# One program order for all engines, idle products in round 0, and a longer reach for the weights, in a linear-attention and MLP kernel

## The chip, the cores and the metric

The kernel runs on one core of a Trainium2 chip. The metric is the device time of one execution in microseconds; lower is better. Each kernel was run several times beside the kernel before on the same chip.

## The reference, cut to what matters

```python
# r, k, v, w: (4 batches, 8 heads, 768 steps, 48); u: (8, 48)
for t in range(S):
    cur = einsum('bhd,bhe->bhde', u[None] * kt, vt)
    y[:, :, t] = einsum('bhd,bhde->bhe', rt, state + cur)
    state = wt[:, :, :, None] * state + einsum('bhd,bhe->bhde', kt, vt)
x = y.transpose(0, 2, 1, 3).reshape(B, S, 384)
xn = (x - mean) / sqrt(var + 1e-06) * g_ln
out = x + maximum(xn @ w_ch1, 0.0) @ w_ch2      # 384 x 1536 and 1536 x 384, handed over as float64
```

## The kernel before

The work is cut into eight rounds of 384 steps, each of two units of four heads. The recurrence of a round is done in six levels. At each level TensorE multiplies r by k (`a_ps`), then VectorE scales r and k by products of w ("scalings", `grow` in the changed kernel) and keeps a part of `a_ps` by a predicated copy. After the levels come the states (`kv`, `s`), the outputs `y`, a normalization, and the MLP of the round: twelve steps for the first matrix (`h_ps`) and twelve for the second (`o_ps`). The MLP of a round runs on TensorE in the gaps of the next round's levels. A stretch of the loop with one level and its share of MLP steps is called a slot.

The weights come as 64-bit floats in 24 parts of 384 columns, and the kernel makes 32-bit floats of their bits. That is a *conversion*: ScalarE makes two halves, VectorE joins them with three operations, and a last integer add finishes the part.

```python
def weights():                                   # a generator; convert(n) takes n steps of it
    for i, (dst, _) in enumerate(parts):
        fetch(i + 2)                             # DMA of the raw part, three buffers
        ...
        ACT.activation(out=e, in_=hi, func=AF.Abs, scale=2.0**-16)
        ACT.activation(out=low, in_=lo, func=AF.Copy, scale=2.0**-29)
        DVE.tensor_scalar(...)                   # clamp
        DVE.tensor_scalar(...)                   # shift, and
        DVE.scalar_tensor_tensor(...)            # sign
        POOL.tensor_tensor(out=dst.bitcast(I32), in0=e, in1=low, op=ALU.add)
        yield
# ... round 0:
for lev in range(NLEV):
    level(now, lev)
    ...
    convert(2)                                   # 12 of the 24 parts, before the first MLP
# ... later rounds, after each slot:
    convert(3)
```

Only TensorE's instructions are held in program order. The scheduler of the framework places those of the other engines.

## Time and profile before

| stage | length, us | from the trace |
|---|---|---|
| round 0, to the first h_ps | 85.4 | TensorE's clock 0.67 |
| first MLP, to the first h_ps of the second | 96.5 | TensorE busy 88.3 |
| the rest | 446.2 | TensorE full |

The median was 631.82 us, and the profiled span 628.1. The page's first part gives busy time, share of the span and number of instructions of each engine. The view of ScalarE's waits in the second stage has what was waited for, the total in us, how often, and the longest wait:

```profile
PE 573.4 (91%) x8456; PEld 387.2 (62%) x8456; DVE 303.2 (48%) x683; ACT 185.2 (29%) x402; POOL 152.4 (24%) x205
```

```profile
ACT h L475 <- PE h_ps L56: 13.7, 6, 6.3
...
ACT wl L212 <- POOL w_sb L225: 5.5, 1, 5.5
```

ScalarE mostly waits for TensorE's products, which here is no loss. Its half conversion (`wl`) waited for a buffer once.

### The profile page before, as it was taken

Reading aid. Unit: us, or ns where it says so; the run is one execution under the profiler, and the core shown is the slowest. Engines: PE = TensorE matmul, PEld = TensorE weight load, DVE = VectorE, ACT = ScalarE, POOL = GpSimd, SP = SyncE. Lnnn points to the kernel's source line nnn. Section 1 sums busy time; section 2 is a strip of 40 time slices with the busy share of each in tenths; the row PEclk is TensorE's granted clock in tenths of the full one; section 3 lists DMA queues with packets and bytes.
Section 4 is the critical chain, followed back from the end, with each engine's and each line's share of the span. In section 5 each row is a group of like instructions: output and inputs, shape, how many; then the busy total and the mean of one; then the engine's idle time right before and its main releaser. Section 6 shows DMA issues by size and latency. Waiting matters only on the chain.

```text
span 628.1 us, 19238 instructions
## 1 busy us (share of the span) xinstructions
PE 573.4 (91%) x8456; PEld 387.2 (62%) x8456; DVE 303.2 (48%) x683; ACT 185.2 (29%) x402; POOL 152.4 (24%) x205
## 2 busy tenths in 40 slices
PE   5366597989999999999999999999999999999997
PEld 4255465656656766667667666676666666566554
DVE  1598959867563544452646356355226361231000
ACT  4108426352143311531243213331142004301200
POOL 7666737670160013300330005101030000000000
PEclk9556769889999989999999999998999999999999
DMA  7656766803410342013400341002000000000000
GB/s 134 144 105 190 182 124 175 183 14 77 91 48 1 59 94 47 15 39 74 88 15 12 68 99 38 1 16 46 26 15 3 15 15 14 1 15 25 1 13 25
DMA packets 123251, 36.83 MB, mean 59 GB/s; under 512 B 116896, under 2 KB 120096, under 8 KB 123168
## 3 DMA queue, kind: packets, MB, share of 16 engines
q1 hardware_dynamic: 121568, 35.32, 25.4%
q8 instruction: 66, 1.08, 0.7%
q10 hardware_dynamic: 1600, 0.30, 0.3%
q14 instruction: 17, 0.14, 0.1%
HBM read 30.87 MB, written 4.72 MB: 57 GB/s over the span
## 4 chain that ended last, share of the span: by engine, by line
PE 82%; DVE 8%; issue 3%; DMA 2%; POOL 2%; SPq 2%; ACT 1%; POOLq 0%; DVEq 0%; ACTq 0%
PE h_ps L56 30%; PE o_ps L56 29%; PE a_ps L56 10%; PE y L56 4%; PE kv L56 2%; PE r_ps L59 2%; PE kn_ps L59 2%; SPq L112 2%; DVE we L221 1%; PE w_ps L59 1%; PE xT_ps L59 1%; DMA nat_r<-in_r_dram 1%; DVE kT L309 1%; PE k_ps L59 1%; DVE rT L309 1%
## 5 line engine op out<-in xcount | busy, mean ns | idle before, releaser
L56 PE MATMUL h_ps<-xT,w_sb 128*128 128x384 f32 x576 | 202.1, 499 | 2.2 <-ACT h L475 2.2
L56 PE MATMUL o_ps<-w_sb,h 128*128 128x384 f32 x576 | 201.2, 495 | 0.0
L56 PEld LDWEIGHTS h_ps<-xT,w_sb 128*128 128x128 f32 x576 | 107.3, 194 | 66.5 <-issue 4.2
L56 PEld LDWEIGHTS o_ps<-w_sb,h 128*128 128x128 f32 x576 | 106.4, 194 | 61.3 <-issue 3.0
L56 PE MATMUL a_ps<-rT,kT 48*64 48x32 f32 x4608 | 86.8, 229 | 25.8 <-DVE kT L309 20.2
L56 PEld LDWEIGHTS a_ps<-rT,kT 48*64 48x64 f32 x4608 | 81.2, 146 | 37.4 <-issue 19.7
L475 ACT ACTIVATE h<-h_ps 128x384 f32<-128x384 f32 x96 | 47.0, 489 | 114.6 <-PE h_ps L56 111.7
L487 DVE TENSOR_TENSOR o<-o_ps,x 128x384 f32<-128x384 f32 x24 | 13.3, 556 | 118.3 <-PE o_ps L56 118.3
L280 POOL TENSOR_TENSOR vo<-v,own 128x576 f32<-128x576 f32 x16 | 19.5, 1221 | 196.1 <-DMA v<-in_v_dram 123.9
L309 DVE TENSOR_TENSOR kT<-kT,tot 128x384 f32<-128x384 f32 x80 | 60.2, 752 | 0.0
L323 DVE COPY_PREDICATED A<-mask,a_ps 128x384 f32<-128x384 int8 x80 | 54.6, 751 | 0.0
L309 DVE TENSOR_TENSOR rT<-rT,tot 128x384 f32<-128x384 f32 x80 | 49.9, 623 | 4.3 <-PE a_ps L56 2.1
L374 DVE SCALAR_TENSOR_TENSOR s<-s,decay,kv 128x48 f32<-128x48 f32 x160 | 30.4, 258 | 43.7 <-PE kv L56 43.7
L421 DVE TENSOR_TENSOR x<-y,vo 128x576 f32<-128x576 f32 x16 | 12.1, 757 | 61.6 <-PE y L56 61.6
L225 POOL TENSOR_TENSOR w_sb<-we,wl 128x384 int32<-128x384 int32 x24 | 33.7, 1416 | 25.6 <-DVE we L221 22.5
L264 POOL TENSOR_TENSOR rk<-nat_k,nat_r 128x576 f32<-128x576 f32 x16 | 27.1, 1691 | 36.1 <-DMA nat_r<-in_r_dram 17.3
L275 DVE TENSOR_REDUCE own<-rk 128x12 f32<-128x576 f32 x16 | 12.0, 749 | 46.5 <-POOL rk L269 46.5
L460 ACT ACTIVATE xT<-xT_ps,g_sb 128x384 f32<-128x384 f32 x24 | 13.9, 580 | 58.5 <-PE xT_ps L59 58.5
L241 ACT COPY rT<-r_ps 128x384 f32<-128x384 f32 x32 | 14.6, 477 | 50.7 <-PE r_ps L59 50.7
L241 ACT COPY kT<-k_ps 128x384 f32<-128x384 f32 x32 | 14.8, 478 | 43.9 <-PE k_ps L59 43.8
L56 PEld LDWEIGHTS y<-v,A 64*64 64x64 f32 x384 | 21.8, 138 | 8.1 <-issue 7.1
L255 POOL TENSOR_TENSOR tot<-wT 128x384 f32<-128x384 f32 x16 | 14.6, 911 | 46.9 <-DVE kT L309 46.8
(57 smaller groups left out, 591.1 us busy)
## 6 DMA issues: line engine op xcount, KB each, us to landing
raw<-in_moe_w_ch_dram SPq DMA_DIRECT2D x24, 384.0 KB, 3.7
nat_w<-in_w_dram SPq DMA_DIRECT2D x64, 72.0 KB, 2.5
nat_k<-in_k_dram SPq DMA_DIRECT2D x64, 72.0 KB, 2.5
v<-in_v_dram SPq DMA_DIRECT2D x64, 72.0 KB, 2.8
out_dram<-o SPq DMA_DIRECT2D x24, 192.0 KB, 2.0
nat_r<-in_r_dram SPq DMA_DIRECT2D x60, 72.0 KB, 2.4
vx<-in_v_dram SPq DMA_DIRECT2D x64, 36.0 KB, 2.3
nat_r<-in_r_dram ACTq DMA_DIRECT2D x4, 72.0 KB, 3.7
```

The source lines that it names most:

```text
L56: tc.keep_in_program_order(PE.matmul(*args, **kw))
L59: tc.keep_in_program_order(PE.transpose(*args))
L225: POOL.tensor_tensor(out=dst.bitcast(I32), in0=e, in1=low, op=ALU.add)
L241: ACT.copy(out=a[nm][:, ts(pr, RN)], in_=ps)
L255: POOL.tensor_tensor(out=t, in0=pair[:, :, 0], in1=pair[:, :, 1], op=ALU.mult)
L264: POOL.tensor_tensor(out=rk, in0=nat["k"][q % 2][:, :, :, 0:D], in1=nat["r"][q % 2][:, :, :, 0:D], op=ALU.mult,)
L280: POOL.tensor_tensor(out=a["vo"], in0=vn[q], in1=o[:, :, :, None].broadcast_to([P, NH, TT, D]), op=ALU.mult,)
L309: DVE.tensor_tensor(out=X, in0=X, in1=T[:, :, 1 - i][:, :, None].broadcast_to(blocks), op=ALU.mult,)
L323: DVE.copy_predicated(out=out_j[:, :, :, 1, :], mask=mask, data=ps_j)
L374: DVE.scalar_tensor_tensor(out=s[:, pr, m, :], in0=s[:, pr, m - 1, :] if m else before[:, pr, 2 * TT - 1, :], scalar=a["T"][NLEV][:, c : c ...
L460: ACT.activation(out=xTs[rnd][:, kc, :], in_=ps, func=AF.Copy, scale=g_sb[:, kc : kc + 1])
L475: ACT.activation(out=hs[f], in_=ps, func=AF.Relu)
```

## The change

Its intent: let no scheduler decide an order, keep TensorE's clock up in round 0 by products of zeros, take the products with u off round 0's path, and ask for the weights further ahead. Cut to its core:

```diff
-    PE, ACT, DVE, POOL, SP = nc.tensor, nc.scalar, nc.vector, nc.gpsimd, nc.sync
+    PE, ACT, DVE, POOL = (
+        InOrder(tc, e) for e in (nc.tensor, nc.scalar, nc.vector, nc.gpsimd)
+    )
+    praw = ctx.enter_context(tc.tile_pool(name="praw", bufs=5))       # raw parts, was 3
...
+    def begin():                       # ScalarE's half of a conversion
+            low[i] = p2.tile([P, WC], I32, tag="low", name=f"low{i}") # two buffers
+            ACT.activation(out=parts[i][0], in_=hi.bitcast(F32), func=AF.Abs, scale=2.0**-16)
+            ACT.activation(out=low[i], in_=lo, func=AF.Copy, scale=2.0**-29)
+    def join():                        # VectorE's half, then the next fetch
...
-            POOL.tensor_tensor(out=dst.bitcast(I32), in0=e, in1=low, op=ALU.add)
+            DVE.tensor_tensor(out=bits, in0=bits, in1=low.pop(i), op=ALU.add)
+    def warm(n):                       # n idle products of zeros
+        ps = ps_m.tile([P, RN], F32, tag="m", name="idle")
+        for _ in range(n):
+            PE.matmul(ps[:, 0:P], nought, nought, start=True, stop=True)
...
-    for lev in range(NLEV):
-        level(now, lev)
-        convert(2)
+    for lev in range(1, NLEV):
+        for q in (u0, u1):
+            quads(q, lev)
+        warm(3 if lev in (3, 4) else 10)
+        ...                            # grow, keep; no conversion
...
+    PARTS = (2, 2, 2, 3, 3, 3, 3, 3)
+            if slot < len(PARTS):
+                tasks += [begin, join] * PARTS[slot]
```

Also, the load of u moves to ScalarE's queue, behind that of the first r, which was there before; the products with u and the totals of w of rounds 0 and 1 move to VectorE, totals are made for both units in one instruction, and some copies of x go. Three parts instead of twelve are converted before the first MLP.

## The prediction

> **What bounds the kernel now.** I read the page's slices first, then busy time by stage, then the timeline of the first 30 us, and last the chain of waits for the pace of TensorE.
>
> The slices (40 of 15.7 us each) give the shape:
>
> ```profile
> PE   5366597989999999999999999999999999999997
> DVE  1598959867563544452646356355226361231000
> PEclk9556769889999989999999999998999999999999
> DMA  7656766803410342013400341002000000000000
> ```
>
> TensorE is full from the tenth slice on; before that it has gaps, and its clock is granted at 0.5 to 0.7 in slices 2 to 6. The stages, cut where the first product of each MLP (h_ps) starts:
>
> ```profile
> core 0: us, PE busy (x) PEld busy (x) DVE busy (x) ACT busy (x) POOL busy (x), PEclk, DMA share, GB/s
> 0.00:85.40 85.40, 47.81 (x1038) 39.45 (x1038) 58.31 (x119) 33.31 (x70) 55.33 (x87) 0.67 0.68 151
> 85.40:181.90 96.50, 88.25 (x1582) 60.83 (x1582) 69.45 (x140) 35.89 (x80) 44.83 (x38) 0.92 0.47 103
> ...
> 253.60:320.70 67.10, 67.10 (x1070) 45.42 (x1066) 33.40 (x75) 20.13 (x45) 13.41 (x18) 1.00 0.25 51
> ```
>
> The second number is the stage's length. So there are three parts: a prologue of 85.4 us (round 0) with no MLP beside it; 96.5 us in which round 1 and most of round 2 run beside the first MLP and the weights are converted; and 628.1 - 181.9 = 446.2 us that TensorE fills by itself.
>
> Why the prologue is slow shows in the timeline:
>
> ```profile
> 16.06 1.40 POOL L269 TENSOR_TENSOR rk<-rk,u_bc 128x576 f32<-128x576 f32 x1 [1.88 <-DMA u_bc<-in_u_dram]
> 17.49 0.75 DVE L275 TENSOR_REDUCE own<-rk 128x12 f32<-128x576 f32 x1 [13.32 <-POOL rk L269]
> ...
> 23.48 0.75 DVE L275 TENSOR_REDUCE own<-rk 128x12 f32<-128x576 f32 x1 [5.23 <-POOL rk L269]
> 24.14 0.55 DVE L309 TENSOR_TENSOR rT<-rT,wT 128x384 f32<-128x384 f32 x1
> ...
> 25.25 1.51 PE L56 MATMUL a_ps<-rT,kT 48*64 48x32 f32 x48 [9.13 <-DVE kT L309]
> ```
>
> Columns: start, length, engine, and in brackets the idle time before it with what ended it. r and k were ready at about 15 us (the first a_ps ran at 14.5), but VectorE stood behind two reductions, whose inputs GpSimd made from u, which landed only at 16 us. The first scaling therefore starts at 24.1, about 9 us late, and TensorE has cooled down by then.
>
> **Pace of TensorE.** At full clock the chain shows this:
>
> ```profile
> 578.18 23.22 PE h_ps L56 x72
> ```
>
> Two records are one product, so 36 products of 384 columns take 23.22 us, 0.645 each; a whole MLP takes 46.5 us, one of its 24 steps 1.94. From the steady stage's timeline: a level of a_ps (96 records) 1.4 to 1.5, y 1.5 per unit, kv 0.73, three transposes 0.33. A full round is then 46.5 + 9 + 3 + 1.5 + 19 x 0.33 = 66.3 us, against 67.1 measured. The steady part has nearly nothing to give.
>
> **What the skill says.** "TensorE: Matmul & The Clock Gate", Part 1: the array's clock is halved by default and comes to full rate only after about 3.4 us of sustained work; the table at its head calls the queues of VectorE, ScalarE and GpSimd strict FIFOs. The trace agrees: a level takes 2.79 us at clock 0.50 (29.9 us) and 1.39 at 1.00. That zeros count as work no run shows yet; I assume it. "SBUF — State Buffer", Who interferes with whom: a VectorE instruction with two SBUF inputs contends with a GpSimd one that reads SBUF. The trace agrees: the kT scaling takes 0.55 us alone, and 1.50 (at 25.6 us) with GpSimd's vo beside it. "VectorE: DVE Perf Modes", tier table: fp32 tensor_tensor runs at rate 1, tensor_scalar at 2. On 384 elements the trace has 0.55 against 0.36; back to back they start 0.47 and 0.27 apart, and those pitches I use below.
>
> **Part 1, the prologue (estimate 62.5 us instead of 85.4).** GpSimd keeps only constants and masks. Rough clock, each engine in its order:
> - TensorE starts about 1 us. An idle product has 128 of 384 columns: 0.215 us at full clock, 0.43 at half. 14 of them end near 7. Six groups (0.33) with 4 idle ones (0.86) end near 13.7, and level 0 of unit 0 is done at 14.5. Unit 1: 0.9 + 6 x (0.33 + 0.65) + 0.75 ends at 22; 12 idle ones, 24.6.
> - VectorE makes r*k*u of unit 0 itself (0.67 x 3 = 2 us, done by 11, as u now comes on ScalarE's queue straight after r), then scales unit 0 and 1 at 14.5 and 22.
> - Each level: VectorE 4 scalings and 2 predicated copies, 6 x 0.47 = 2.8; TensorE 1.5 + 10 x 0.215 = 3.65. So the idle products, not VectorE, pace levels 1, 2 and 5; levels 3 and 4 have transposes instead and take 3.2. Level 5 is issued at 38.5. Before, its products started at 44.6.
> - From there: level 5 and its ten idle ones to 42; ends and copies to 46; own products of unit 1 on VectorE 2; two states of 12 steps at 0.19 = 2.3 each, to 50.6; own terms 1.4, y sums, one conversion, moments to 57; norm, two conversions to 62. First MLP product about 62.5.
> 138 idle products cost 29.7 us of TensorE at full clock, nearly all in time when it would wait. They add perhaps 2 us where they hold back work that is ready (before level 1, before kn).
>
> **Part 2, round 1 and most of round 2 (estimate 101 us instead of 96.5).** Here I think the change loses. TensorE has 24 steps (46.5), 10 levels (15), y and kv 4.5, 24 groups of w, k, r, 4 of kn, 3 of xT (10): about 76 us. But VectorE gets more: before, half of the weights were converted during the prologue; now only 3 of 24 are. A conversion is 0.27 + 0.27 + 0.47 plus the integer add that GpSimd did, taken as 0.47: 1.5 us (the add is an own instruction over 768 half-words; if it takes twice that, 2). 21 of them are 31 us, in the first 8 of 11 slots. With 8 x 2.8 of scaling, the own terms of round 1 (2 x 2.7), totals (2.1), states (4) and sums, these 8 slots have 67 us on VectorE and 52 on TensorE.
> As every queue is in order, they also wait for each other. I followed both queues with these durations. Slots 0 and 1: VectorE does totals to 64.6, level 0 and own products of one unit to 69.5, two conversions to 72.5, level 1 and the other unit's products to 77.5, part 5 at 79. TensorE has done h_ps 0 to 2 and level 1's a_ps by 70 and waits 9 us for part 5, as h_ps 3 needs parts 3 to 5; it cools, and hands VectorE level 2 only at 84, some 4 us late. Slot 2 ends on VectorE at 90, slot 3 (three conversions, an own term) at 98, slot 4 at 106, slot 5 at 114. Slots 6 and 7 (2.3 of states, 2.8 and 4.5 each) end at 124 and 134: the last conversion. The o_ps step that needs it ends at 138. Three slots of TensorE are left: 7 steps (13.6), 3 levels (4.5), two y (3), 8 groups (2.7), xT (1), together 25. So the second MLP starts at 163, which is 101 us after the first.
>
> **Part 3 (446 us, unchanged).** Rounds stay bound by TensorE. Totals for both units in one instruction save starts on GpSimd, which idles; the copies of x (3 x 0.35 a round) leave VectorE, which is half idle. VectorE now waits in order for GpSimd's products at level 5: about 10 us of chain before level 1 of the next round, some 20 us later. Nothing gained, nothing lost.
>
> **Sum.** 62.5 + 101 + 446 = 609.5 us of span. Before, span 628.1 was 629.8 in that run and 631.8 at the median: add 2 to 3. I take out 2 for better fetches and stalls I have counted twice, and predict 610.
>
> **Rivals.**
> 1. VectorE does not stall in part 2: the 8 slots take their 67 us, part 2 is 92, the time 601. For it: GpSimd's conflicts are gone (its 44.8 us busy there falls to some 10). Against: joins, relus and products in three fixed queues.
> 2. Weights arrive late. The raw parts stand in one queue behind loads that wait for transposes; DMA was 0.68 busy over the prologue, and now most of 9.4 MB comes after it. Each such wait of 2 to 3 us moves the end; five make 620. For it: ScalarE already waited 25.5 us for raw in the first 190. Against: five parts in flight instead of three.
> 3. Zeros don't keep the clock up, or the idle products are late and become the bound: a level at half clock is 3 + 4.3 = 7.3, five levels cost 18 us more, and the prologue gains nothing: 630.
> 4. A steady stage that loses 1 us a round to order: +7.
>
> **Range and chances.** Rivals 1 and 2 are likeliest: 600 to 622. Faster by over 2% (below 619.2) 0.84, within 2% 0.15, slower 0.01.
>
> **What would show it.** Right: first h_ps near 62, clock 1.00 from about 8 us through the prologue, level 5 at 38 to 40; VectorE over 80% busy from there to 130 and the second MLP's start at 155 to 168; 446 after it. Wrong: clock 0.50 in the prologue (rival 3); raw as what ends ScalarE's waits (rival 2); a conversion well over 1.5; or rounds other than 67 to 70.

## The result

The changed kernel took 657.51 us at the median of four runs (656.27 to 659.04), the kernel before 633.51 beside it. The ratio is 1.0375, 95% interval 1.0309 to 1.0442: slower by 3.7%, where I had predicted 610. A ratio here and below is the mean time of one kernel's runs over the mean of the other's of the same rounds, so it is not quite the ratio of the quoted medians. Executions over 1.5% slower than the fastest of the same kernel are left out of the means.

The page of the changed kernel, parts 1 and 2 (a slice is now 16.4 us):

```profile
PE 603.7 (92%) x8732; PEld 414.5 (63%) x8732; DVE 307.9 (47%) x724; ACT 186.4 (28%) x402; POOL 79.9 (12%) x109
...
PE   9998856657699999999999999999999999999997
...
DVE  3666987576635554446352725353443552212000
...
PEclk9999868788599999999999999999999999999999
```

The clock is high early: zeros do keep it up. (The profile has no clock record for the first 6 us and counts them as full, as it does the first 12.0 us of the kernel before. The records of idle products start 0.21 us apart until 6.0 us and 0.11 after, so the clock was half until then. It stood at 1.00 from 6.0 to 64.0 us, and at 0.50 for the 6.8 us after that.) The weak part has moved. It is now slices 5 to 11, the first MLP, and VectorE is not full there either. Busy time by stage, cut as in the prediction:

```profile
core 0: us, PE busy (x) PEld busy (x) DVE busy (x) ACT busy (x) POOL busy (x), PEclk, DMA share, GB/s
0.00:71.20 71.20, 66.00 (x1313) 61.93 (x1314) 44.86 (x104) 23.86 (x51) 9.42 (x37) 0.95 0.65 130
71.20:215.10 143.90, 103.88 (x1587) 67.82 (x1586) 94.75 (x203) 45.81 (x100) 14.62 (x14) 0.79 0.39 91
215.10:282.85 67.75, 67.33 (x1051) 45.56 (x1050) 31.91 (x79) 20.27 (x44) 11.67 (x12) 1.00 0.25 50
```

Round 0 gave 14.2 us (85.4 to 71.2), the second stage took 47.4 (96.5 to 143.9), and the rest, 657.3 - 215.1 = 442.2, gave 4. So the whole loss is in the second stage, in which TensorE idles for 40 us and VectorE for 49. One slot of it, from the timeline (start, length, engine, instruction, and in brackets the idle time before it with what ended it):

```profile
104.05 0.56 DVE L48 TENSOR_TENSOR rT<-rT,tot 128x384 f32<-128x384 f32 x1 [1.52 <-PE a_ps L48]
...
106.65 0.82 PE L48 MATMUL w_ps<-ident,nat_w 128*128 128x128 f32 x6
...
109.01 0.56 DVE L48 CUSTOM_DVE_ANT_0 w_sb<-w_sb,low 128x768 uint16<-128x768 uint16 x1
109.48 0.75 DVE L48 TENSOR_SCALAR w_sb<-w_sb 128x384 f32<-128x384 f32 x2
109.60 0.56 ACT L48 ACTIVATE low<-raw 128x384 int32<-128x384 uint32 x1 [4.55 <-DVE w_sb L48]
110.06 0.47 ACT L48 ACTIVATE h<-h_ps 128x384 f32<-128x384 f32 x1
...
112.01 0.83 ACT L48 COPY wT<-w_ps 128x384 f32<-128x384 f32 x2
...
112.52 1.14 PEld L48 LDWEIGHTS w_ps<-ident,nat_w 128*128 128x128 f32 x6 [5.29 <-ACT wT L48]
112.52 1.54 PE L48 MATMUL w_ps<-ident,nat_w 128*128 128x128 f32 x6 [5.05 <-DMA raw<-in_moe_w_ch_dram]
...
113.86 4.05 PE L48 MATMUL h_ps<-xT,w_sb 128*128 128x384 f32 x6
...
117.83 1.94 PE L48 MATMUL a_ps<-rT,kT 48*64 48x32 f32 x96
...
119.15 0.56 DVE L48 TENSOR_TENSOR rT<-rT,tot 128x384 f32<-128x384 f32 x1 [5.68 <-PE a_ps L48]
```

This is read from the middle. At 109.60 ScalarE's `low` had stood for 4.55 us until VectorE's add (`CUSTOM_DVE_ANT_0`, the integer add on half-words) was done at 109.57: `low` has two buffers, and the add releases the one from two parts back. Behind it, in the same queue, stood the relu of an h_ps and the copies of `w_ps`. TensorE had no free transpose buffer until the first of these copies (112.01), so it idled for 5.05 us; for the products the profile names a DMA of raw, which a transpose doesn't read; for the weight loads of the same transposes (`PEld`) it names ScalarE's copy. TensorE had cooled by then: six records of h_ps (three products, two records each) take 4.05 us at 113.86, at a granted clock of 0.50, and 2.20 at 104.61, at 1.00. So the next a_ps came late, and VectorE waited 5.68 us for it. VectorE and TensorE take turns, through ScalarE. The next slots repeat this at 119.15 and 133.81. The waits in the whole stage say the same, ScalarE's first, then TensorE's:

```profile
ACT low L48 <- DVE w_sb L48: 48.4, 12, 9.6
```

```profile
PE o_ps L48 <- DVE w_sb L48: 10.0, 6, 4.9
PE h_ps L48 <- DVE w_sb L48: 8.0, 1, 8.0
PE r_ps L48 <- ACT rT L48: 7.5, 2, 7.3
PE k_ps L48 <- DMA raw<-in_moe_w_ch_dram: 5.4, 1, 5.4
PE w_ps L48 <- DMA raw<-in_moe_w_ch_dram: 5.1, 1, 5.1
```

A wait of the kind that took 5.5 us in the kernel before now takes 48.4. Of TensorE's 40 us, some 18 are waits for its transposes, behind ScalarE (the last three lines). But another 18 are waits for converted weights (`w_sb`) themselves, which more buffers need not mend. No wait of ScalarE or VectorE in this stage is for a raw part. That gave the theories for the experiments: (A) ScalarE's place in the middle, (B) the amount of work on VectorE, (C) weights late by DMA, (D) VectorE's fixed order, and later (E) the lack of slack between a join and the step that needs it.

### The profile page after: what moved, and what is told of

Same layout as the page of the kernel before. It is cut to its first block, busy times and chain, and to the rows that moved or that the text cites. A ratio compares the mean times of both kernels' runs of the same rounds, so it can differ in the third digit from the quotient of the medians.

```text
span 657.3 us, 19673 instructions
## 1 busy us (share of the span) xinstructions
PE 603.7 (92%) x8732; PEld 414.5 (63%) x8732; DVE 307.9 (47%) x724; ACT 186.4 (28%) x402; POOL 79.9 (12%) x109
## 4 chain that ended last, share of the span: by engine, by line
PE 85%; DVE 8%; DMA 2%; SPq 2%; issue 1%; ACT 1%; DVEq 0%; ACTq 0%
PE h_ps L48 28%; PE o_ps L48 28%; PE a_ps L48 10%; PE idle L48 5%; DVE w_sb L48 4%; PE y L48 3%; PE kv L48 2%; PE w_ps L48 2%; PE k_ps L48 2%; PE r_ps L48 2%; PE kn_ps L48 2%; SPq L123 2%; PE xT_ps L48 1%; DVE A L48 1%; DMA raw<-in_moe_w_ch_dram 1%
## 5 line engine op out<-in xcount | busy, mean ns | idle before, releaser
L48 PEld LDWEIGHTS a_ps<-rT,kT 48*64 48x64 f32 x4608 | 77.1, 141 | 15.7 <-issue 14.3
L48 PE MATMUL a_ps<-rT,kT 48*64 48x32 f32 x4608 | 81.9, 224 | 4.0 <-issue 4.0
L48 POOL TENSOR_TENSOR vo<-v,own 128x576 f32<-128x576 f32 x12 | 13.9, 1155 | 338.7 <-DVE own L48 338.7
L48 DVE TENSOR_TENSOR rT<-rT,tot 128x384 f32<-128x384 f32 x80 | 43.6, 554 | 17.7 <-PE a_ps L48 17.7
L48 DVE TENSOR_TENSOR kT<-kT,tot 128x384 f32<-128x384 f32 x80 | 44.2, 553 | 9.1 <-PE a_ps L48 8.3
L48 DVE TENSOR_TENSOR x<-y,vo 128x288 f32<-128x288 f32 x32 | 13.1, 452 | 62.5 <-PE y L48 62.5
L48 PE MATMUL idle<-nought 128*128 128x128 f32 x276 | 39.6, 297 | 1.1 <-DVE eps L48 1.1
L48 PEld LDWEIGHTS idle<-nought 128*128 128x128 f32 x276 | 36.3, 209 | 1.6 <-DVE eps L48 1.1
L48 ACT ACTIVATE low<-raw 128x384 int32<-128x384 uint32 x24 | 13.2, 552 | 50.6 <-DVE w_sb L48 50.6
L48 POOL TENSOR_TENSOR rk<-nat_k,nat_r 128x576 f32<-128x576 f32 x12 | 17.0, 1417 | 77.0 <-DMA nat_k<-in_k_dram 76.7
```

The source lines that it names most:

```text
L48: return lambda *args, **kw: self.tc.keep_in_program_order(f(*args, **kw))
```

## The experiments

All 17 runs gave correct outputs. "First h" is the start of the first h_ps, "stage" the time from there to the first h_ps of the second MLP, both of the profiled run; "rest" is the remainder of its span.

| kernel | first h | stage | rest | median, us | ratio to before, 95% |
|---|---|---|---|---|---|
| before | 85.3 | 96.5 | 446.3 | 631.8 | |
| changed | 71.2 | 143.8 | 442.3 | 657.5 | 1.0375 (1.0309 to 1.0442) |
| e_low4 | 69.3 | 128.4 | 440.9 | 642.5 | 1.0168 (1.0112 to 1.0223) |
| e_actfree | 77.5 | 129.2 | 447.1 | 655.2 | 1.0368 (1.0320 to 1.0415) |
| e_pe | 88.5 | 99.0 | 446.4 | 638.2 | 1.0097 (1.0020 to 1.0173) |
| e_nowarm | 58.8 | 150.0 | 443.7 | 654.2 | 1.0363 (1.0306 to 1.0419) |
| e_low4_pooladd | 66.8 | 133.6 | 443.7 | 646.1 | 1.0208 (1.0123 to 1.0292) |
| e_low4_dvefree | 79.8 | 115.7 | 441.8 | 640.2 | 1.0123 (1.0048 to 1.0197) |
| e_low4_levels | 62.9 | 128.6 | 443.3 | 640.2 | 1.0113 (1.0011 to 1.0214) |
| e_switch4 | 72.9 | 124.2 | 453.3 | 652.0 | 1.0303 (1.0224 to 1.0383) |
| e_early1 | 70.1 | 110.4 | 447.5 | 627.8 | 0.9923 (0.9873 to 0.9972) |
| e_early2 | 80.7 | 97.4 | 445.4 | 624.5 | 0.9880 (0.9805 to 0.9955) |
| b_late | 77.4 | 107.2 | 443.0 | 630.8 | 0.9973 (0.9913 to 1.0033) |
| b_own | 93.6 | 97.1 | 446.9 | 634.4 | 1.0037 (0.9976 to 1.0097) |
| e_only_early2 | 85.0 | 107.2 | 441.1 | 634.9 | 1.0077 (1.0013 to 1.0141) |
| e_early2_nowarm | 79.4 | 102.3 | 447.0 | 631.9 | 1.0033 (0.9963 to 1.0102) |
| e_early2_pool | 80.5 | 97.8 | 444.5 | 624.6 | 0.9928 (0.9861 to 0.9994) |
| e_early2_pairs | 77.2 | 97.5 | 444.1 | 622.2 | 0.9892 (0.9806 to 0.9979) |
| e_loads | 72.6 | 97.6 | 449.7 | 616.6 | 0.9779 (0.9720 to 0.9839) |

### e_low4: four low buffers

```diff
-            low[i] = p2.tile([P, WC], I32, tag="low", name=f"low{i}")
+            low[i] = p4.tile([P, WC], I32, tag="low", name=f"low{i}")
-    praw = ...(name="praw", bufs=5)    # RAW = 5
+    praw = ...(name="praw", bufs=4)    # RAW = 4, to pay for it
```

> The changed kernel with four buffers instead of two for low (the half of a conversion that ScalarE makes ahead), paid for with four raw buffers instead of five; nothing else moves. Theory A (ScalarE, in order, stands at its second copy until VectorE has joined the part two before it; relus and PSUM copies stand behind it, so TensorE and VectorE take turns in each slot): ScalarE's waits of low for VectorE, 48.4 us between the two MLP starts, fall below 15; that stage shrinks from 143.9 to 105 to 120 us and the time to 620 to 635. Theory B (VectorE has too much work in a fixed order, and weights are late whatever ScalarE does): low no longer waits, but TensorE still waits for w_sb, and the stage stays above 135, the time above 648. Theory C (weights arrive late by DMA): one raw buffer less makes it worse, above 660.

ScalarE's wait of `low` for VectorE is gone from the list, and the kernel is 15 us faster at the median, most of it from the stage (15.4 us there). So theory A is right that this wait costs, but its size was too large: 642.5 and a stage of 128 lie between the numbers of A and B. Theory C fell: with one raw buffer less, the kernel is faster. ScalarE does wait for raw parts now (20.7 us in nine waits of the stage), but VectorE waits nowhere in it for ScalarE's half, so no join is late by them. What is left in the stage, in TensorE's timeline:

```profile
143.45 1.65 PE L48 MATMUL o_ps<-w_sb,h 128*128 128x384 f32 x2 [7.41 <-DVE w_sb L48]
145.40 1.65 PE L48 MATMUL o_ps<-w_sb,h 128*128 128x384 f32 x2 [0.31 <-DVE w_sb L48]
147.36 1.65 PE L48 MATMUL o_ps<-w_sb,h 128*128 128x384 f32 x2 [0.31 <-DVE w_sb L48]
```

TensorE waits for a part joined a moment ago, takes it, and waits for the next: one product every 1.95 us, which is the length of a join, where 0.645 would do at full clock.

### e_actfree: ScalarE's order left to the scheduler

```diff
+    ACT = nc.scalar
```

> The changed kernel with ScalarE alone released from program order (the scheduler places its instructions; the queue is then as fixed as before, only its order is another). Theory A: the relus and PSUM copies are put ahead of the waiting half conversions; the stage between the MLP starts shrinks from 143.9 to 105 to 125 us, the time is 620 to 640. Theory B: nothing changes by more than 1%, 650 to 660.

The stage shrank by 14.6 us, close to what four buffers gave, but the first h_ps came 6.3 us later and the rest was 4.8 longer; at the median 2 us were left. The time is in the range of theory B, the stage in that of neither. The wait of `low` was not removed either (27.2 us in the stage, still 12 times). Releasing one engine from order is not a clean experiment: the scheduler also moved what had stood well.

### e_pe: program order on TensorE alone

```diff
+    ACT, DVE, POOL = nc.scalar, nc.vector, nc.gpsimd
```

> Program order on TensorE alone, as in the kernel before; all other parts of the change stay (idle products, five raw parts asked for ahead, integer adds and own terms on VectorE, totals of both units). If order on the three other engines is the cause of the loss (A): 615 to 635. If it is the work moved to VectorE and the conversions moved out of round 0 (B): 645 or more, with the stage between the MLP starts above 130 us.

The stage fell to 99, but the first h_ps came at 88.5. The trace shows what went with it: twelve parts had been joined by then, against three in the changed kernel. At 638.2 neither range of times was met; as the conversions came early again, the two theories are not separated by it.

### e_nowarm: no idle products

```diff
     def warm(n):
+        n = 0
+        if not n:
+            return
```

> The changed kernel without its 138 idle products. If they earn what I predicted, the granted clock in the first 71 us falls from 0.95 to about 0.7, each level of round 0 takes about 1.3 us longer, and the first h_ps comes 6 to 14 us later, near 80; the second stage is as long as before or a little longer, so the time is 663 to 673. If idle products hold back as much as they give, the time stays within 654 to 660.

The opposite of my expectation: without them the first h_ps comes 12.4 us *earlier*, at 58.8 (the time, 654.2, is in the second of the ranges), though the granted clock of round 0 is lower:

```profile
0.00:58.80 58.80, 43.97 (x1038) 36.34 (x1039) 41.16 (x98) 23.87 (x51) 9.40 (x37) 0.77 0.66 132
```

In the changed kernel, the timeline of TensorE shows idle products filling its queue completely between two levels:

```profile
25.69 1.60 PE L48 MATMUL a_ps<-rT,kT 48*64 48x32 f32 x96
27.22 2.50 PE L48 MATMUL idle<-nought 128*128 128x128 f32 x20
29.65 1.60 PE L48 MATMUL a_ps<-rT,kT 48*64 48x32 f32 x96
```

Inside the levels they do earn something: from level 3 to level 5 it takes 41.25 - 33.61 = 7.6 us with them and 36.15 - 26.06 = 10.1 us without, at the lower clock. But 72 idle products stand ahead of level 1, and level 3 starts at 33.6 us instead of 26.1; 40 more follow the last a_ps, and from level 5 to the first h_ps it takes 71.2 - 41.25 = 30.0 us with them and 58.8 - 36.15 = 22.6 without. Later the stage became 6 us longer, so only 3 us were left at the end.

### On top of e_low4: the add, VectorE's order, the idle products, order in round 0 alone

Theories B and D each predicted a gain from one of these:

```diff
 e_low4_pooladd:  -DVE.tensor_tensor(out=bits, in0=bits, in1=low.pop(i), op=ALU.add)
                  +POOL.tensor_tensor(out=bits, in0=bits, in1=low.pop(i), op=ALU.add)
 e_low4_dvefree:  +DVE = nc.vector
 e_low4_levels:   idle products in levels 1 to 5 only (36 of 138)
 e_switch4:       e_low4_levels, and ACT, DVE, POOL out of program order from the first MLP on
```

> On top of e_low4 (four low buffers): the integer add of every conversion goes back to GpSimd, as in the kernel before. In e_low4 VectorE is busy for nearly all of the 92 us from the first h_ps (69.3) to the last join (161.2), and TensorE waits 25.6 us for converted weights. Theory B (the amount of work on VectorE): one join takes 0.6 to 0.7 us less of it, 21 joins 12 to 15 us; the stage between the MLP starts falls from 128.3 to 115 to 120 us, the time from 642.5 to 628 to 634. Theory D (it is the fixed order, not the amount): no more than 3 us. If GpSimd's add conflicts with VectorE's scalings, the gain is lost: 640 or more.

> On top of e_low4: VectorE released from program order, the work on it unchanged; ScalarE, GpSimd and TensorE stay in order. Theory D (the fixed order of VectorE): the stage between the MLP starts falls from 128.3 to 105 to 112 us, the time to 620 to 628. Theory B (the amount): within 1% of e_low4's 642.5.

> On top of e_low4: idle products only inside levels 1 to 5 of round 0 (36 of the 138); the other 102 left out. They took 22 us of TensorE at full clock, and I now think that most of it stood ahead of ready work: the first h_ps comes at 54 to 60 instead of 69.3. If the second stage is bound by VectorE's 92 us of work from there, the second MLP starts 10 to 12 us earlier too, time 629 to 634; if by something with a date of its own (weights by DMA), the stage gets longer by as much and the time stays at 638 to 643.

> e_low4_levels with program order on ScalarE, VectorE and GpSimd in round 0 only; from the first MLP on they are free, as in the kernel before (TensorE stays in order). If order after round 0 is what costs (A and D together): first h_ps at 56 to 62, the stage between the MLP starts near the 99 us of e_pe, 443 after it: 602 to 612, faster than both kernels. If the conversions moved out of round 0 are what costs, order or not (B): stage 120 or more, time 625 or more.

None of these met the number of the theory that it was made for. With the adds on GpSimd, the last join came *later* (164.0 instead of 161.2), and TensorE waited 27.4 us for GpSimd's adds. I had named this outcome, and the trace shows what I had feared: beside an add of GpSimd, VectorE's own instructions take longer. The pair of clamp and shift that takes 0.75 us above takes 1.44 here:

```profile
105.39 1.44 DVE L48 TENSOR_SCALAR w_sb<-w_sb 128x384 f32<-128x384 f32 x2
105.62 0.99 POOL L48 TENSOR_TENSOR w_sb<-w_sb,low 128x384 int32<-128x384 int32 x1 [5.76 <-ACT wT L48]
```

Of the 24 shifts, 14 took 1.05 us instead of 0.36. So VectorE's busy time from the first h_ps to the last join fell only from 82.8 to 77.3 us, where I had counted on 12 to 15 less, and this run doesn't refute B; e_early1 and e_early2 below do. VectorE out of order shortened the stage by 12.7 and lengthened round 0 by 10.5; its time, 640.2, was in B's range. Fewer idle products brought the first h_ps 6.4 us earlier, and about 2 us reached the median, within the noise; the stage stayed as long as it was. Order in round 0 alone lost: the stage went down only by 4 us against e_low4_levels, and round 0 and the rest both got longer by 10. In round 0 TensorE waits 12.0 us there for the normalized x of VectorE, a wait that e_low4_levels doesn't have: the scheduler had placed other work first. Stage (124.2) and time (652.0) are those named for late conversions, order or not. So D fell too, as the whole cause.

The table suggested something else. Before these runs, all kernels with a long stage had one to three parts converted when the first MLP began, and those with a short one (before, e_pe) twelve. In the changed kernel each step of the first MLP takes parts that are joined in its own slot. VectorE joins them after that slot's scalings; the next scalings wait for an a_ps that stands in TensorE's queue behind the step. With no slack between a join and its step, a microsecond taken off one engine should only let the other wait. That is theory E.

### e_early1 and e_early2: conversions back in round 0

```diff
-        if lev == 2:
-            begin()
+        run([begin, join] * 1)         # e_early2: * 2; after each of the six levels
```

> On top of e_low4_levels: one more conversion after each of the six levels of round 0, so that 9 parts instead of 3 are ready when the first MLP starts. Theory E (slack: each step of the first MLP uses parts that are joined only in its own slot, after that slot's scalings, and those scalings wait for products queued behind the step; VectorE and TensorE take turns. In the runs so far the stage took 124 to 150 us with 3 parts ready, and 96 to 99 with about 12): the first h_ps comes 6 to 10 us later, at 69 to 73, the stage shrinks from 128.6 to 105 to 112, time 622 to 632. Theory B (only the amount of VectorE work counts): what round 0 gains in length the stage loses, 636 to 642, as e_low4_levels.

> The same with two conversions after each level, 15 parts ready. Theory E: first h_ps at 78 to 84, stage 92 to 98, time 618 to 630. Theory B: 636 to 645. If raw parts cannot arrive that fast in round 0, VectorE or ScalarE waits for raw there and the first h_ps is later than 88.

Both met theory E's numbers in every place: first h_ps at 70.1 and 80.7, stage 110.4 and 97.4, time 627.8 and 624.5. By stage, e_early2:

```profile
0.00:80.70 80.70, 53.89 (x1110) 46.00 (x1111) 62.97 (x149) 34.90 (x75) 9.47 (x37) 0.80 0.76 169
80.70:178.10 97.40, 87.58 (x1585) 59.96 (x1585) 72.38 (x157) 34.04 (x76) 15.58 (x14) 0.94 0.41 90
```

Against e_low4_levels, round 0 is 17.8 us longer and the stage 31.2 shorter. TensorE waits for w_sb no more in it. VectorE's work up to the second MLP is about the same (135 us; 142 there), so B, by which the time would have stayed at 636 or more, fell here: twelve joins made round 0 17.8 us longer and took 31.2 off the stage.

### b_late and b_own: the same from the other side

```diff
 b_late, on the kernel before:
-            convert(2)                 # in each level of round 0
+    convert(3)                         # once, before the first MLP
-            e = ph.tile(..., tag="h", ...)     # and low; 13 buffers in ph
+            e = p2.tile(..., tag="we", ...)    # and low, tag="wl"; 12 in ph
 b_own: the last two lines alone
```

> The kernel before, with its conversions taken out of round 0's levels (three are left before the first MLP, three follow in each slot, as in the changed kernel) and its two temporaries in buffers of their own, without which it would deadlock. Nothing else of the change. Theory E: the stage between the MLP starts grows from 96.5 to 120 or more, round 0 gets shorter by 5 to 15 us, time 640 to 660. If the loss of the changed kernel comes from program order or idle products instead, this costs little: 625 to 636.

> Control of b_late: the kernel before with the two temporaries of a conversion in buffers of their own (two each) and nothing else. Within 1% of before, 626 to 638.

By the note made before the run, b_late without the separate buffers would deadlock. Against b_own, late conversions make the stage 10 us longer (107.2, not the 120 of E) and round 0 16 us shorter; the medians are 630.8 and 634.4. So in the kernel before, with the adds and products on GpSimd and three engines free to be reordered, converting late costs nothing, though five parts, not three, were joined before the first h_ps here. The time is in the range that I had named against theory E. That sets a bound on it: lateness hurt only together with something else of the changed kernel, such as the fixed order or the fuller VectorE. No run separates these two.

### The last five: what is still open after e_early2

```diff
 e_only_early2:   the changed kernel with the early conversions of e_early2 and nothing else
 e_early2_nowarm: e_early2 without its 36 idle products
 e_early2_pool:   e_early2 with the adds on GpSimd
 e_early2_pairs:  e_early2 with two parts joined instruction by instruction:
+        for x in v:    DVE.tensor_scalar(...)              # clamp of both
+        for x in bits: DVE.tensor_scalar(...)              # shift of both, and so on
 e_loads:         e_early2_pairs with
-    for q in (u0, u1):                 # before level 0
-        load_v(q)
-        load_vx(q)
+        if lev == 2:                   # the same three lines here
```

> The changed kernel with twelve more conversions in round 0 (two after each level) and nothing else: two low buffers, five raw, all 138 idle products. If the two low buffers cost only because joins stood late in each slot, the slack mends it by itself: first h_ps at 84 to 90, stage 96 to 102, time 624 to 634. If ScalarE's wait of low holds TensorE back whatever the slack: stage 108 to 118, time 636 to 648.

> e_early2 (624.5) without its 36 idle products. If they earn what they seemed to inside the levels (about 1.1 us each of five levels), the first h_ps comes 3 to 7 us later and the time is 627 to 632. If VectorE's joins pace the levels now, so that TensorE's clock there no longer matters: 622 to 626.

> e_early2 with the integer adds on GpSimd. A join takes about 1.3 us of VectorE instead of 1.95. If VectorE's work binds round 0, the first h_ps comes up to 8 us earlier and the time is 615 to 621; if GpSimd's adds slow VectorE's two-input instructions beside them, as its products did in the kernel before, or the weights come later for the longer way round, 624 to 634.

> e_early2 with the joins of two parts interleaved instruction by instruction, so that no instruction waits for the result of the one just before it. If the 1.95 us of a join is dependency (pitches of 0.27, 0.27, 0.47 and 0.47, which I had summed to 1.5, plus 0.1 to 0.2 at each handover), two take 3.0 to 3.2 instead of 3.9, round 0 is 4 to 6 us shorter and the time is 616 to 621. If the instructions simply take that long, nothing changes: 622 to 627.

> e_early2_pairs (622.2) with the loads of v and its exchanged copy for units 0 and 1 issued after level 2 of round 0 instead of before level 0. If the 8.0 us that VectorE waits there for parts 4 and 5 are the path: first h_ps at 68 to 71 instead of 77.2, the stage 97 to 99 as before, time 613 to 617, over 2% faster than the kernel before. If v then comes late, or raw is late anyway because the transfers and not their order bind: 619 to 626.

**e_only_early2** came to 634.9, just between the two ranges, with a stage of 107.2. So the slack alone takes 22.6 us off the changed kernel's median (657.5), and its ratio to before falls from 1.0375 to 1.0077. The two low buffers still cost: ScalarE still waits 28.7 us for VectorE's joins between 60 and 190 us. **e_early2_nowarm** was 7.4 us slower at the median than e_early2 (ratio to before 1.0033 against 0.9880), though its first h_ps came no later (79.4 and 80.7); its stage was 4.9 us longer. So the 36 products inside the levels are worth something, but not where I thought, and why the stage gains is open. **e_early2_pool** changed nothing (624.6); VectorE's busy time up to the second MLP didn't fall either (138.4 us, 135.4 with the adds on VectorE).

**e_early2_pairs** measures the join. In VectorE's timeline two parts take 24.33 - 21.35 = 2.98 us:

```profile
21.35 1.19 DVE L48 TENSOR_SCALAR w_sb<-w_sb 128x384 f32<-128x384 f32 x4
22.45 1.02 DVE L48 SCALAR_TENSOR_TENSOR w_sb<-raw,w_sb 128x384 int32<-128x384 int32 x2
23.39 1.02 DVE L48 CUSTOM_DVE_ANT_0 w_sb<-w_sb,low 128x768 uint16<-128x768 uint16 x2
24.33 0.55 DVE L48 TENSOR_TENSOR rT<-rT,tot 128x384 f32<-128x384 f32 x1
```

That is 1.49 each, as I had summed it from the pitches (the times from one start to the next); in a row, each instruction waiting for the one before, a join takes 1.95 (109.01 to 110.96 in the changed kernel). Round 0 became 3.5 us shorter, a little less than expected, and the whole time doesn't show it: the ratios of 0.988 without and 0.989 with pairs don't tell the two apart. In the same trace VectorE waits in round 0 for ScalarE's halves of parts 4 and 5:

```profile
DVE w_sb L48 <- ACT w_sb L48: 8.0, 2, 5.9
```

Their raw data were asked for at 35.24 us, behind the 16 loads of v. **e_loads** moves those loads; the wait falls to 1.0, the first h_ps comes at 72.6 (expected 68 to 71), and the median is 616.6 over six runs (616.4 over the five fast ones). The profiled run was one of its slowest (621.6; they went from 612.7 to 622.2), so its "rest" of 449.7 says little. This version beats both kernels: 2.2% faster than before, interval 1.6 to 2.8%. Whether it is more than 2% is left unclear by that interval; that it is faster is not.

## Why the prediction was wrong, point by point

The predicted span was 609.5 us, the profiled one 657.3. Part 1 has 8.7 of the difference, part 2 42.8, and part 3 took 3.7 less than I had.

**Part 1, the prologue: the mechanism was half right, and one term had the wrong sign.** The clock held, as assumed, until 64 us. Level 5 was issued at 41.3 where I had 38.5, and the first h_ps at 71.2 where I had 62.5. A level with ten idle products took 3.96 us (25.69 to 29.65) where I had 3.65; a level at full clock alone is 1.53 (25.69 to 27.22), and not the 1.39 that I had read. The step that failed is "they add perhaps 2 us where they hold back work that is ready". Without idle products the first h_ps came 12.4 us earlier. The gain in round 0 came from elsewhere: round 0 was shorter than before without any idle product. By how much each of the earlier load of u, the moved products with u, and the missing conversions did it, no run here separates; b_late shows 16 us for the conversions alone in the kernel before.

**Part 2, the first MLP: here the prediction failed.** I had 101 us and it took 143.8. The step is "I followed both queues with these durations": I followed VectorE and TensorE and left out ScalarE's queue, although the change puts it in order too. Through the two low buffers ScalarE was tied to VectorE's joins, with relus and copies behind it. Four buffers gave 15.5 us back. The second failed step is the slack. I did write that TensorE waits 9 us for part 5 in slots 0 and 1, but counted it once; three converted parts are the number that the first steps use up, and such waits came back: seven in the changed kernel (18.0 us), nine with four low buffers (25.6 us). I had named the loss of the early conversions (three parts instead of twelve) only as added work on VectorE. Twelve more, put back into the levels, shorten the stage by 36.6 us in the changed kernel and the time by 22.6. The two gains overlap: with both, and the idle products cut, the kernel went from 657.5 to 624.5.

The size of a term was off as well. A conversion was put at 1.5 us, "if it takes twice that, 2" for the add. The add itself has a pitch of 0.47; the join is 1.95 because its four instructions depend on each other. For 21 joins that is 9 us more than the 31 I had, and from the first h_ps to the last join VectorE was busy 78 us where I had 67. In the changed kernel VectorE's last join then came at 179 us where I had 134, and from there to the second MLP it took 35 us instead of 29.

**Part 3** was right: 442.3 where I had 446, so rival 4 fell.

**Rivals.** Rival 1 (VectorE doesn't stall) fell: from the first h_ps to the last join 108 us went by and not 67. Up to 130 us VectorE was busy 78% of the time, just under the 80% that I had named; over the whole stage, 66%. Rival 2 had the right symptom, weights that come late, but named the wrong queue: they were late from VectorE's joins, not from the DMA. Rival 3 fell on the clock, but came near in its other half, "the idle products are late and become the bound". None of the rivals was the one that happened, a third engine that makes the other two take turns. I gave "slower by over 2%" one chance in a hundred, which was far too little for a change that fixes the order of four queues at once.

**What the skill said.** From the table at the head of the Trainium skill's "TensorE: Matmul & The Clock Gate" I had cited that ScalarE's queue is a strict FIFO, and did not use it. The trace shows it: a relu whose product was ready at 106.8 stood behind `low` until 110.06. The Trainium skill's page "Perfetto Trace Analysis", section Optimization Strategy, says that the same gap repeating on an engine that should be full can mean that there are too few buffers for the next tile. The trace agrees in part: the gap that repeats is that of ScalarE before `low` (12 times, 48.4 us), and four buffers ended it; TensorE, the engine that should be full, idled behind it (5.05 us in the slot shown). Still, the buffers were only part of it (15 us of the median): the larger part was how late the joins stood (22.6).

## What to carry to other kernels

Before fixing the order on an engine, follow its queue to the first instruction that waits for another engine, and list what stands behind it; a ring of two buffers in a queue that also empties PSUM, the memory that TensorE writes to, can tie three engines together, as it did here. Leave slack between a producer and its consumer when both run in order: the same work done a few slots earlier took 36.6 us off the stage, while moving the adds off the busy engine took nothing, because beside GpSimd's adds its own instructions took longer. Idle work that keeps a clock up belongs only where the engine waits for certain, because in an in-order queue it delays what is ready.

## What the Trainium skill lacked or had wrong

- "TensorE: Matmul & The Clock Gate", Part 1, does not say whether products of zeros count as work for the clock gate. They do: nothing but idle products ran from 1.1 to 6.6 us, and at 6.0 the distance of their records fell from 0.21 to 0.11 us. Over round 0 the granted clock is 0.95 with them and 0.77 without, where the first 6.0 and 11.2 us have no record and count as full. Nor does it say what they cost in the way of ready work: 12.4 us here.
- "VectorE: DVE Perf Modes", section The DRAIN you can't avoid, has that a semaphore after each of eight copies cost nothing extra (it does not say that they read each other's results). Here four dependent instructions took 1.95 us, and 1.49 with another part's instructions between them: 0.46 us a chain for waiting on one's own results.
- No page that I found has the duration of an exact 32-bit integer add on VectorE. The trace has it as an own instruction on 768 half-words: 0.56 us for 384 numbers, a pitch of 0.47, the same as an fp32 multiplication of two tensors of that length.
- No page that I found says that a predicated copy depends on the length of its runs (mask, data and output have the same). Two of 384 columns took 1.85 us at levels 0 and 1 (runs of one and two elements) and 1.02 from level 2 on (runs of four and more).
